# Attention into a soft mixture of experts: a new order of the last weight tiles, a finer warming-up, and one normalisation moved from VectorE to ScalarE

## The chip, the cores and the metric

The kernel runs on one core of a Trainium2 chip. The core has five engines, each with its own instruction queue: TensorE (PE, matmuls and their weight loads), VectorE (DVE), ScalarE (ACT), GpSimd (POOL) and SyncE (SP), which here issues nearly all DMA transfers. The metric is the device time of one execution in microseconds (us); lower is better. Times inside an execution are counted from the start of its span.

## The reference

Attention over 8 batches of 8 heads with 576 tokens and 64 channels, and a soft mixture of experts on its output:

```python
q_rot, k_rot = rotate(q), rotate(k)
scores = scale * q_rot @ k_rot.T
attn = softmax(scores)            # over keys, 1e-9 added to the sum
x = (attn @ v) -> (4608, 512)     # 8 x 576 tokens, 8 heads x 64
logits = x @ phi                  # 32 slots, 4 for each of 8 experts
d = softmax(logits, over tokens)
slot_input = d.T @ x
slot_out[e] = relu(slot_input[e] @ w1[e]) @ w2[e]     # 512 -> 1024 -> 512
out = softmax(logits, over slots) @ slot_out
```

The arrays are float32. The two softmaxes over the logits need all tokens of all batches (the one over tokens) or can be done batch by batch (the one over slots).

## The kernel before, in words

**Attention.** The 64 heads are worked off as 32 pairs, numbered 0 to 31; four pairs make a batch. A pair's q and k come in (`x_in`), are multiplied by cosines and sines on GpSimd (line 226), added on VectorE, and split into a high and a low float16 half (`hl`). PE multiplies them once for the row maxima (line 281, reduced on VectorE, line 283) and once for the scores (line 357), ScalarE takes the exponential into `a_t` and `a_tr` (lines 358, 376, 377), and PE multiplies that with V (line 392), whose last column of ones gives the sums. `o_out` copies the result to `o_sb`, `recip` takes one over the sums, and `norm` multiplies by it on GpSimd (line 441) into `xn`, the tokens of the batch.

**Order.** The order in which these steps are emitted is written out by hand: the list `FRONT`, then times in `EARLY` and `WHEN`. A step's time has no unit and only sorts the steps; each engine then works through its own instructions in that order, waiting on semaphores. GpSimd and SP follow the same order. Pair 29's `norm` stands at 141.9, after pair 30's at 140.1.

**The end of attention.** `release_att` closes the memory pools of attention and lays eleven weight tiles of 512 KB, `wt0` to `wt10`, over them; `FREED` is the order in which they are loaded. By the order of the pools `wt0` and `wt1` lie over the two `o_sb` and pair 30's `v_in`, `wt2` over pair 31's `v_in` and the first `a_t`, `wt3` to `wt6` over the four `a_t`, `wt7` over the last `a_t`, `a_tr` and pair 30's `hl`, `wt8` and `wt9` over the `hl` of pairs 30 and 29, and `wt10` over that of pair 31. SP issues one load after the other, so a load whose memory is still in use holds up those behind it. The weights themselves come in the same order whichever tile they go to.

Then the pairs of the last batch are transposed (`natural`, line 465: nine transposes a pair, into a bank each), copied to `xt` (`natural_out`, line 485) and multiplied with phi (line 491). Pair 31 is normalised straight from PSUM by `norm_last`, all on VectorE, its last 64 queries of each head by line 456; `natural_last` (lines 474 to 477) transposes it into the bank that `natural_out(30)` has emptied and a second one.

**Experts.** Statistics of the last batch and the update of the slot inputs (lines 526 to 908), the two layers (`ffn1_steps`, line 921, and `ffn2_steps`, line 943), and the combination with the tokens' weights (line 973), whose results go out from line 976 on.

**Warming-up.** While the first loads run, `heat` sends matmuls to PE whose result nobody reads: 21 of 288 columns, each with its own weight load (line 737). A second call sends 16 more.

Of the kernel before, what the change touches and what calls it, by code (L numbers as in the profile page):

```python
# [26 lines left out]
HC = S // 2  # L27
# [12 lines left out]
)  # L40
N_WARM = 21
N_ROW = 2
FIRST = 1
N_COLD = 3
# [9 lines left out]
N_HL = 3  # L54
N_XN = 1
WIDE = True
FREED = (9, 8, 10, 3, 4, 5, 6, 0, 1, 7, 2)
PACE = {("m_rows", 29): 3, ("m_rows", 30): 3, ("m_rows", 31): 1}
WHEN = {
    "load0": (-18.089368, -21.237240, -19.262252, -19.815526), "spin0": (-18.026370, -19.323083, -15.395919,  # L60
# [88 lines left out]
}  # L149
QL, QH, KH, KL = range(4)  # L150
TERMS = ((KH, QH), (KH, QL), (KL, QH), (None, None))
# [3 lines left out]
def attn_softmoe(ctx, tc, qk, v, phi, w1, w2, cs, ident, sel, seg, out):  # L155
    nc = tc.nc
# [22 lines left out]
    rows = (slice(0, 64), slice(64, P))  # L179
# [7 lines left out]
    lift = const.tile([P, P], F16, name="lift")  # L187
# [21 lines left out]
    halves = {}  # L209
# [43 lines left out]
    def bank2(k=None):  # L253
        if k is None:
            k = min((i for i in range(N_S) if age[i] is not None), key=lambda i: age[i])
        age[k] = None
        t = ps[k].tile([P, 2, 512], F32, name=f"s_ps{k}")
        held[id(t)] = k, t
        return t

    def free(t):
        k, _ = held.pop(id(t))
        age[k] = next(ages)
# [120 lines left out]
    def av(p, i):  # L384
        if i == 0:
            os_[p] = bank2()
            left_av[p] = NB + 1
        o, vt, at = os_[p], vts[p], ats.pop((p, i))
        left_av[p] -= 1

        def unit(lhs, c, h, u, v):
            nc.tensor.matmul(o[rows[c], h, VW * u:VW * u + VW], lhsT=lhs, rhs=v, start=(i == 0 and u == 0),  # L392
                             stop=(left_av[p] == 0 and u == 3 + (c == h)))

        if i < NB:
            for c, h, u in [(c, h, u) for u in range(4) for h in range(2) for c in range(2)] + [(0, 0, 4), (1, 1, 4)]:
                q = 256 if u == 4 else 64 * u + 320 * c
                unit(at[:, h, q:q + 64], c, h, u, vt[:, 2 * i + h])
        else:
            for u in range(5):  # L400
                for c in range(2):
                    for r in range(2 if u < 4 else 1):
                        q = 256 if u == 4 else 64 * u + 320 * c
                        q += 64 * (r ^ c)
                        unit(at[rows[r], q:q + 64], c, r ^ c, u, vt[rows[r], 2 * NB + c])
# [37 lines left out]
    def norm_last(p):  # L443
        t = os_.pop(p)
        free(t)
        o = t[:, :, 0:5 * VW].rearrange("p h (u x) -> p h u x", x=VW)
        rr, pp = rrs[p % 2], p % NP
        nc.vector.tensor_scalar_add(out=rr[:, :, 0:4], in0=o[:, :, 0:4, 64], scalar1=1e-9)
        for h in range(2):
            nc.vector.tensor_scalar_add(out=rr[rows[h], h, 4:5], in0=o[rows[h], h, 4, 64:65], scalar1=1e-9)  # L450
        nc.vector.reciprocal(out=rr, in_=rr)
        xn = xns[p // NP][:, :, pp * P:(pp + 1) * P].rearrange("p j (h x) -> p h j x", h=2)
        nc.vector.tensor_tensor(out=xn[:, :, 0:4], in0=o[:, :, 0:4, 0:64],
                                in1=rr[:, :, 0:4].unsqueeze(3).broadcast_to([P, 2, 4, 64]), op=ALU.mult)
        for h in range(2):
            nc.vector.tensor_scalar_mul(out=xn[0:64, h, 4], in0=o[rows[h], h, 4, 0:64], scalar1=rr[rows[h], h, 4:5])

    def natural(p, k=None):
        b, pp = divmod(p, NP)
# [21 lines left out]
    def natural_out(p):  # L481
        xts[p] = xt = late.tile([P, S], F32, name="xt", bufs=N_X)
        t = flat.pop(("n", p))
        free(t)
        nc.scalar.copy(out=xt, in_=t.rearrange("p n x -> p (n x)")[:, 192:192 + S])  # L485
# [160 lines left out]
    def load_w(pool, bufs, tag="w_exp", pace=None, wt=None):  # L646
        n = order[len(w_tiles)]
        layer, rest = divmod(n, 4 * E)
        if wt is not None:
            wt = wt.rearrange("p (c x) -> p c x", c=4 if layer else 2)  # L650
        elif layer == 0:
            wt = pool.tile([P, 2, 512], F32, name=tag, bufs=bufs)
        else:
            wt = pool.tile([P, 4, 256], F32, name=tag, bufs=bufs)
        if pace is nc.vector:
            pace.memset(wt[0:1, 0, 0:1], 0.0)
        elif pace:
            before = w_tiles[order[len(w_tiles) - 2]]
            pace.tensor_copy(out=wt[0:1, 0, 0:1], in_=before[0:1, 0, 0:1])
        nc.sync.dma_start(out=wt.rearrange("p c x -> p (c x)"), in_=(w1, w2)[layer][rest])  # L660
        w_tiles[n] = wt
# [13 lines left out]
    def release_att():  # L675
# [5 lines left out]
        wt.append(tl.tile([P, 1024], F32, name="wt10"))  # L681
        for i in FREED:
            load_w(None, 1, wt=wt[i])
# [46 lines left out]
        plan[f"t{i}"] = lambda p, i=i: score(p, i)  # L730
    for i in range(NB + 1):
        plan[f"av{i}"] = lambda p, i=i: av(p, i)
    def heat(n):
        cold = bank2()
        free(cold)
        for _ in range(n):
            nc.tensor.matmul(cold[:, 0, 0:HC], lhsT=lift, rhs=halves[0][:, KH, 0:HC], start=True, stop=True)

    def small_loads(p):
        nc.sync.dma_start(out=phi_sb, in_=phi.rearrange("(c p) n -> p c n", p=P))  # L740
        nc.sync.dma_start(out=sel_sb, in_=sel)

    plan.update({
        "heat": lambda p: heat(16),
        "small_loads": small_loads,
        "join0": lambda p: join(p, 0),
# [23 lines left out]
            high(0, t, c)  # L770
    done.update((n, 0) for n in ("spin0", "spin1", "join", "high0", "high1", "load0", "load1"))
    done.update((n, 1) for n in ("join0", "join1"))
    heat(N_WARM)

    last = NPAIR - 1
    STEADY = {n: w if isinstance(w, tuple) else (w,) * NP for n, w in WHEN.items()}
# [26 lines left out]
    natural(last - 1, 1)  # L803
    natural(last - 3, 0)
    norm_last(last)
    for q in (last - 2, last - 1, last - 3):
        natural_out(q)
    lt = bank2(2)
    lp = lt[:, 0, 0:192]
# [28 lines left out]
    m, al, dt, xn = state["m"], state["al"], state["dt"], xns.pop(B - 1)  # L838
# [28 lines left out]
    for c in range(2):  # L867
        for j in range(4):
            nc.tensor.matmul(sh[c][32 * j:32 * j + 32], lhsT=dn[:, 32 * j:32 * j + 32],
                             rhs=xn[:, j, 256 * c:256 * c + 256], start=True, stop=True, tile_position=(0, 32 * j))  # L870
    for i in range(NP):
        nc.tensor.matmul(rp[32 * i:32 * i + 32], lhsT=dn[0:64, P + 32 * i:P + 32 * i + 32],
                         rhs=xn[0:64, 4, i * P:(i + 1) * P], start=True, stop=True, tile_position=(0, 32 * i))
# [32 lines left out]
    for _ in range(N_LEAD):  # L906
        load_w(wp, N_W)
    nc.vector.tensor_tensor(out=st[:, 0:256].rearrange("p (i e z) -> p i e z", i=NP, z=2 * SPE)[:, :, :, SPE:],
                            in0=fp[:, 0:P].rearrange("p (i e z) -> p i e z", i=NP, z=SPE),
# [171 lines left out]
```

## Time and profile before

| | us |
|---|---|
| median of 3 runs | 482.27 |
| lowest, highest run | 481.59, 484.14 |
| profiled execution, its own time | 483.52 |
| its span, first to last instruction | 481.7 |
| PE busy | 457.9 (95%) |
| VectorE, ScalarE, GpSimd busy | 374.9, 291.1, 289.8 |

The profiled execution is one run; its time is its span and what lies around it (1.8 us). Busy times are sums over the span. The chain that ended last is followed back from the last instruction to whatever released each one. "issue" is time in which an engine waited for nothing that the profile shows. `q8` is the DMA queue whose packets are called "instruction".

### The profile page before, as it was taken

To read this page: it belongs to the slowest core of one execution; us is meant where nothing else is said; L and a number is where in the kernel's file an instruction comes from. 1 tells how busy PE (TensorE), PEld (TensorE's weight loads), DVE (VectorE), ACT (ScalarE), POOL (GpSimd) and SP (SyncE) were. 2 spreads that over 40 slices of the span, in tenths; PEclk is the share of its full clock that TensorE was granted. 3 is DMA by queue.
4 is the path that set the end of the run, shared out by engine and by line. 5 is a ranking of instruction groups with operands and counts; after the bars stand their busy time and mean duration, and the time that the engine had idled before them with its cause. 6 is when DMAs were issued, how large, how long until landed. Compare 5 with 4: busy or idle time off the path is not lost.

```text
span 481.7 us, 24135 instructions
## 1 busy us (share of the span) xinstructions
PE 457.9 (95%) x10758; PEld 374.2 (78%) x10758; DVE 374.9 (78%) x630; ACT 291.1 (60%) x670; POOL 289.8 (60%) x321
## 2 busy tenths in 40 slices
PE   4699999999999999999999999999999999999992
PEld 2377888878888788878887888888878888853871
DVE  4998998878878887988899889988896864356443
ACT  2166767665676577657765776577666766632442
POOL 2897858947893778577866787687849301230000
PEclk9899999999999999999999999999999999999997
DMA  7545745472554356335543553444452044799898
GB/s 256 194 146 191 257 150 197 168 264 98 197 182 170 123 175 213 122 132 193 196 146 138 199 174 129 148 142 173 167 197 101 23 171 164 254 405 407 342 376 326
DMA packets 29707, 94.00 MB, mean 195 GB/s; under 512 B 5028, under 2 KB 6820, under 8 KB 29604
## 3 DMA queue, kind: packets, MB, share of 16 engines
q1 hardware_dynamic: 29604, 92.47, 53.8%
q8 instruction: 84, 1.38, 1.2%
q14 instruction: 19, 0.16, 0.1%
HBM read 82.95 MB, written 9.44 MB: 192 GB/s over the span
## 4 chain that ended last, share of the span: by engine, by line
PE 90%; DVE 4%; ACT 2%; DMA 1%; issue 1%; SPq 0%; DVEq 0%; ACTq 0%
PE s_ps L392 34%; PE s_ps L357 26%; PE s_ps L281 8%; PE s_ps L372 4%; PE o_ps L943 3%; PE o_ps L921 3%; PE s_ps L465 2%; PE s_ps L502 2%; PE c_ps L973 2%; PE s_ps L290 2%; DVE nm L283 1%; PE s_ps L562 1%; DMA x_in<-in_qk 1%; DVE hl L239 1%; DVE x_in L230 1%
## 5 line engine op out<-in xcount | busy, mean ns | idle before, releaser
L226 POOL TENSOR_TENSOR x_in<-x_in,cs_sb 128x288 f32<-128x288 f32 x248 | 236.8, 987 | 82.7 <-DMA x_in<-in_qk 61.1
L283 DVE TENSOR_REDUCE nm<-s_ps 128x2 f32<-128x576 f32 x256 | 187.6, 752 | 48.9 <-PE s_ps L281 47.7
L392 PEld LDWEIGHTS s_ps<-v_in,a_t 128*64 128x64 f32 x4608 | 139.2, 137 | 12.2 <-issue 4.5
L358 ACT ACTIVATE a_t<-s_ps 128x576 f32<-128x576 f32 x256 | 145.8, 660 | 4.0 <-PE s_ps L357 3.8
L392 PE MATMUL s_ps<-v_in,a_t 128*64 128x66 f32 x4608 | 146.3, 223 | 0.2 <-issue 0.2
L357 PE MATMUL s_ps<-hl 64*128 64x288 f16 x1536 | 133.2, 283 | 0.0
L357 PEld LDWEIGHTS <-hl 64*128 64x128 f16 x1536 | 79.2, 94 | 18.4 <-issue 8.0
L357 PE MATMUL s_ps<-peak,lift 64*128 64x288 f16 x512 | 75.3, 283 | 0.3 <-ACT peak L334 0.3
L281 PE MATMUL s_ps<-hl 64*128 64x288 f16 x512 | 67.0, 286 | 3.2 <-ACT hl L235 1.5
L423 ACT COPY o_sb<-s_ps 128x528 f32<-128x528 f32 x31 | 18.6, 600 | 75.2 <-PE s_ps L392 75.2
L441 POOL TENSOR_TENSOR xn<-o_sb,rr 128x640 f32<-128x640 f32 x31 | 39.7, 1290 | 33.2 <-PE s_ps L562 13.9
L235 ACT CAST hl<-x_in 128x576 f16<-128x576 f32 (+1 forms) x66 | 40.8, 657 | 22.7 <-DVE x_in L230 22.6
L239 DVE TENSOR_TENSOR hl<-x_in,hl 128x1152 f16<-128x1152 f32 x32 | 52.9, 1653 | 1.6 <-ACT hl L235 1.6
L230 DVE TENSOR_TENSOR x_in<-x_in 128x1152 f32<-128x1152 f32 (+1 forms) x35 | 47.4, 1355 | 0.1
L281 PEld LDWEIGHTS <-hl 64*128 64x128 f16 x512 | 29.1, 94 | 18.4 <-issue 7.9
L357 PEld LDWEIGHTS <-lift 64*128 64x128 f16 x512 | 27.0, 94 | 4.9 <-issue 0.5
L292 DVE TENSOR_REDUCE nm<-s_ps 128x2 f32<-128x576 f32 x32 | 24.0, 751 | 3.4 <-PE s_ps L290 3.4
L392 PE MATMUL s_ps<-v_in,a_tr 64*64 64x66 f32 x1152 | 26.4, 224 | 0.0
L392 PEld LDWEIGHTS s_ps<-v_in,a_tr 64*64 64x64 f32 x1152 | 21.9, 133 | 4.3 <-issue 3.5
L372 PE MATMUL s_ps<-hl 64*64 64x256 f16 (+1 forms) x384 | 24.1, 287 | 0.0
L485 ACT COPY xt<-s_ps 128x576 f32<-128x576 f32 x31 | 19.4, 651 | 5.0 <-PE s_ps L465 5.0
L376 ACT ACTIVATE a_tr<-s_ps 128x512 f32<-128x512 f32 x32 | 19.1, 598 | 4.7 <-PE s_ps L372 3.9
(184 smaller groups left out, 419.7 us busy)
## 6 DMA issues: line engine op xcount, KB each, us to landing
x_in<-in_qk SPq DMA_DIRECT2D x62, 576.0 KB
w_exp<-in_w SPq DMA_DIRECT2D x53, 512.0 KB
v_in<-in_v SPq DMA_DIRECT2D x32, 330.0 KB
out<-w_exp SPq DMA_DIRECT2D x16, 512.0 KB
wt<-in_w SPq DMA_DIRECT2D x11, 512.0 KB
peak<-mr SPq DMA_DIRECT2D x120, 0.5 KB
x_in<-in_qk SPq DMA_DIRECT2D x4, 288.0 KB
out<-w_exp SPq DMA_DIRECT2D x4, 256.0 KB
```

Source lines behind the costliest of these rows:

```text
L226: eng.tensor_tensor(out=x[:, :, c], in0=x[:, :, c], in1=cs_sb[:, :, c], op=ALU.mult)
L230: nc.vector.tensor_tensor(out=x[:, t, 0, c], in0=x[:, t, 0, c], in1=x[:, t, 1, c], op=ALU.add)
L235: nc.scalar.copy(out=halves[p][:, 1 + t, c], in_=loaded[p][:, t, 0, c])
L239: nc.vector.tensor_tensor(out=hl[:, 0:4:3], in0=x[:, :, 0], in1=hl[:, 1:3], op=ALU.subtract)
L281: nc.tensor.matmul(s[c, h, 0:HC], lhsT=hl[rows[h], QH, P * j + c.start:P * j + c.stop], rhs=hl[rows[h], KH, half[n]], start=True, stop=True)
L283: nc.vector.tensor_reduce(out=nm[:, n, j:8:4], in_=s[:, :, 0:HC], axis=AX.X, op=ALU.max, negate=True)
L292: nc.vector.tensor_reduce(out=nm[:, :, 8], in_=s[:, :, 0:HC], axis=AX.X, op=ALU.max, negate=True)
L357: nc.tensor.matmul(s[c, h, 0:HC], lhsT=lhs, rhs=rhs, start=(x == 0), stop=(x == 3))
L358: nc.scalar.activation(out=ats[p, b][:, :, half[n]], in_=s[:, :, 0:HC], func=AF.Exp, scale=SCALE)
L372: nc.tensor.matmul(s[rows[h ^ n], n, 0:w] if n else s[rows[h], 0, 512 - w:512], lhsT=lhs, rhs=rhs, start=(x == 0), stop=(x == 3))
L392: nc.tensor.matmul(o[rows[c], h, VW * u:VW * u + VW], lhsT=lhs, rhs=v, start=(i == 0 and u == 0), stop=(left_av[p] == 0 and u == 3 + (c == ...
L441: eng.tensor_tensor(out=xn, in0=t[:, :, :, 0:64], in1=rr.unsqueeze(3).broadcast_to([P, 2, 5, 64]), op=ALU.mult)
```

## The change

1. The first warming-up sends 29 matmuls of 209 columns in place of 21 of 288. The second call keeps its 16 of 288.
2. `FREED` becomes 9, 8, 0, 1, 10, 7, 3, 4, 5, 6, 2, and pair 29's `norm` is emitted at 129.0, before pair 30's and after the steps at 128.3.
3. In `norm_last` the last 64 queries of the second head are multiplied on ScalarE. `natural_out(29)` is emitted ahead of that multiply, so ScalarE's order is `natural_out(29)`, the multiply, `natural_out(30)`, `natural_out(28)`.

```diff
-N_WARM = 21
+N_WARM, W_WARM = 29, 209
...
-FREED = (9, 8, 10, 3, 4, 5, 6, 0, 1, 7, 2)
+FREED = (9, 8, 0, 1, 10, 7, 3, 4, 5, 6, 2)
...
-    ("av1", 31): 140.406591, ("norm", 29): 141.896775, ("av4", 31): 142.290391,
+    ("av1", 31): 140.406591, ("norm", 29): 129.000000, ("av4", 31): 142.290391,
...
-        for h in range(2):
-            nc.vector.tensor_scalar_mul(out=xn[0:64, h, 4], in0=o[rows[h], h, 4, 0:64], scalar1=rr[rows[h], h, 4:5])
+        nc.vector.tensor_scalar_mul(out=xn[0:64, 0, 4], in0=o[rows[0], 0, 4, 0:64], scalar1=rr[rows[0], 0, 4:5])
+        natural_out(p - 2)
+        nc.scalar.mul(out=xn[0:64, 1, 4], in_=o[rows[1], 1, 4, 0:64], mul=rr[rows[1], 1, 4:5])
...
-    def heat(n):
+    def heat(n, w=HC):
...
-            nc.tensor.matmul(cold[:, 0, 0:HC], lhsT=lift, rhs=halves[0][:, KH, 0:HC], start=True, stop=True)
+            nc.tensor.matmul(cold[:, 0, 0:w], lhsT=lift, rhs=halves[0][:, KH, 0:w], start=True, stop=True)
...
-    heat(N_WARM)
+    heat(N_WARM, W_WARM)
...
-    for q in (last - 2, last - 1, last - 3):
+    for q in (last - 1, last - 3):
         natural_out(q)
```

## Rows read from the trace of the kernel before

**Rows 1.** The page: busy time and instructions; DMA queue q8; chain's shares.

```profile
PE 457.9 (95%) x10758; PEld 374.2 (78%) x10758; DVE 374.9 (78%) x630; ACT 291.1 (60%) x670; POOL 289.8 (60%) x321
...
q8 instruction: 84, 1.38, 1.2%
...
PE 90%; DVE 4%; ACT 2%; DMA 1%; issue 1%; SPq 0%; DVEq 0%; ACTq 0%
PE s_ps L392 34%; PE s_ps L357 26%; PE s_ps L281 8%; PE s_ps L372 4%; PE o_ps L943 3%; PE o_ps L921 3%; PE s_ps L465 2%; PE s_ps L502 2%; PE c_ps L973 2%; PE s_ps L290 2%; DVE nm L283 1%; PE s_ps L562 1%; DMA x_in<-in_qk 1%; DVE hl L239 1%; DVE x_in L230 1%
```

**Rows 2.** Timeline of PE, 414 to 428: start, us, operation, count, idle before.

```profile
414.24 4.44 PE L392 MATMUL s_ps<-v_in,a_t 128*64 128x66 f32 x144
...
419.35 0.52 PE L465 MATMUL s_ps<-id_sb,xn 64*128 64x64 f32 x9
420.62 0.78 PE L465 MATMUL s_ps<-id_sb,xn 64*128 64x64 f32 x18 [0.76 <-issue]
...
421.83 0.52 PE L474 MATMUL s_ps<-id_sb,xn 64*128 64x64 f32 x9
...
427.36 0.41 PE L872 MATMUL t_ps<-xn,dn 64*32 64x128 f32 x5 [0.39 <-issue]
```

**Rows 3.** Windows: PE, PEld, DVE, ACT, POOL busy (instructions), clock, DMA share, GB/s.

```profile
420.62:427.36 6.74, 6.31 (x128) 4.42 (x128) 3.46 (x12) 4.10 (x16) 1.95 (x7) 1.00 0.99 393
```

**Rows 4.** DMA queues, 417.50 to 419.40: packets, MB, share of 16 engines.

```profile
q8 instruction: 1, 0.02, 5.8%
```

**Rows 5.** DMA queues, 425.0 to 426.2.

```profile
q8 instruction: 1, 0.02, 5.5%
```

**Rows 6.** Timeline, 100 to 102.

```profile
100.82 0.26 ACT L377 ACTIVATE a_tr<-s_ps 64x128 f32<-64x128 f32 x1
101.61 0.10 PEld L281 LDWEIGHTS <-hl 64*128 64x128 f16 x2 [1.32 <-issue]
```

**Rows 7.** DMA queues, 99.1 to 100.3.

```profile
q8 instruction: 1, 0.02, 5.0%
```

**Rows 8.** Timeline of SP, DMA issues, 95.5 to 98.

```profile
95.54 0.39 SPq L221 DMA_DIRECT2D x_in<-in_qk  x1
```

**Rows 9.** Windows (columns as in rows 3).

```profile
96.49:101.61 5.12, 4.00 (x132) 3.41 (x130) 4.66 (x7) 2.19 (x9) 1.90 (x3) 1.00 0.74 238
```

**Rows 10.** Timeline, 6.5 to 13.

```profile
6.84 4.70 PE L737 MATMUL s_ps<-hl,lift 128*128 128x288 f16 x21 [6.84 <-ACT hl L235]
...
12.75 0.74 DVE L283 TENSOR_REDUCE nm<-s_ps 128x2 f32<-128x576 f32 x1
```

**Rows 11.** Timeline of GpSimd, 398 to 416.

```profile
411.34 2.48 POOL L441 TENSOR_TENSOR xn<-o_sb,rr 128x640 f32<-128x640 f32 x2 [4.92 <-DVE rr L433]
```

**Rows 12.** Timeline of SP, single DMA issues, 405 to 415.

```profile
408.43 0.34 SPq L660 DMA_DIRECT2D w_exp<-in_w  x1
...
414.22 0.33 SPq L660 DMA_DIRECT2D wt<-in_w  x1
```

**Rows 13.** Timeline of ScalarE and VectorE, 419.3 to 423.

```profile
419.90 0.64 ACT L485 COPY xt<-s_ps 128x576 f32<-128x576 f32 x1 [3.83 <-PE s_ps L465]
...
420.82 0.57 DVE L456 TENSOR_SCALAR xn<-s_ps,rr 64x64 f32<-64x64 f32 x2
421.13 1.18 ACT L485 COPY xt<-s_ps 128x576 f32<-128x576 f32 x2 [0.59 <-PE s_ps L465]
```

**Rows 14.** ScalarE's groups by shape, 404 to 482: busy us, mean ns, idle before.

```profile
L425 ACT COPY o_sb<-s_ps 64x66 f32<-64x66 f32 x2 | 0.4, 209 | 0.0
```

**Rows 15.** Timeline of PE, 184.0 to 184.8.

```profile
184.66 0.34 PE L392 MATMUL s_ps<-v_in,a_t 128*64 128x66 f32 x5 [0.16 <-issue]
```

**Rows 16.** Windows (columns as in rows 3).

```profile
18.00:20.00 2.00, 1.93 (x11) 1.00 (x10) 2.00 (x4) 0.00 (x0) 1.08 (x2) 0.50 0.94 351
20.00:22.00 2.00, 2.00 (x13) 1.23 (x10) 2.00 (x3) 1.19 (x2) 1.83 (x2) 0.72 1.04 402
22.00:24.00 2.00, 1.93 (x19) 1.38 (x20) 1.90 (x6) 0.06 (x1) 1.86 (x4) 1.00 0.49 193
```

## The prediction

> **What bounds the kernel now.** I read the page first. TensorE (PE) is busy 95% of the span, and the chain that ended last is 90% PE; the whole DMA share of that chain is 1%, and one entry, the first load of x_in, accounts for it [rows 1]. So no weight tile and no output is waited for in the tail. A change of load order can pay only if it makes PE's own chain shorter. Then I went through PE's timeline for places where PE stands still though nothing that the program waits for is late ("issue"). The two in the tail stand before the 10th transpose of line 465 (0.76 us) and in the middle of line 872 (0.39 us) [rows 2]. The reader should see how far apart they are: from the end of the first to the end of the second PE runs 128 matmuls and 128 weight loads, 256 instructions [rows 3]. The page gives the reason for that number: 10,758 matmuls and as many weight loads, 21,516 instructions, against 84 "instruction" packets of 1.38 MB, which is 256 instructions and 16 KB a packet [rows 1]. PE's program itself comes by DMA in blocks of 256, and PE stalls where a block is late.
>
> The DMA table dates the packets. One fills most of 417.5 to 419.4: 5.8% of 16 engines over 1.9 us is 1.76 us [rows 4]. The next lies in 425.0 to 426.2 and takes 5.5% of 16 times 1.2 us, 1.06 us [rows 5]. PE goes on at 420.62 and 427.36 [rows 2], about 1.25 us after each has ended. The second was due for asking when PE entered the block before, at 420.62, and started only around 425.0: in between the DMA engines were 0.99 busy with weights [rows 3]. A block waits behind weight packets. That is the way by which this change can act.
>
> A third stall shows the same in mid-kernel: PE stands until 101.62. There its next bank was free only when ScalarE's a_tr ended at 100.82 + 0.26 = 101.08, so the block cost 101.61 - 101.08 = 0.53 us [rows 6]. Its packet (5.0% of 16 times 1.2, 0.96 us) lies in 99.1 to 100.3 [rows 7], behind an x_in load issued at 95.54; PE had entered the block before at 96.49, 256 instructions and the few that the window's edges cut in two earlier [rows 8, 9].
>
> **Part 1, the warming-up.** 21 matmuls of 288 columns are 6,048 columns; 29 of 209 are 6,061, 13 more, which is 0.01 us at either clock. Before, they took 4.70 us, until 11.54 [rows 10]. If instead every extra matmul cost as much as a whole old one, 4.70 / 21 = 0.22, the burst would be 8 x 0.22 = 1.8 us longer; if it cost nothing, it would be as long as now. [...] The cover is VectorE, which takes up line 281's bank only at 12.75, 1.2 us after the burst [rows 10]: it hides that much of a longer one, so the upper bound would cost 0.6 us, and without the cover 1.8.
>
> What does act is the count: 8 more matmuls with their loads are 16 more instructions ahead of everything else, so each block of PE's program now ends 16 instructions, 8 matmuls, earlier in the code.
>
> **Part 2, norm 29 earlier on GpSimd, and the weight tiles.** Before, norm(30) and norm(29) run back to back on GpSimd, 2.48 us from 411.34, because norm(30) stood first [rows 11]. Now norm(29) runs when its reciprocal is done, and norm(30) ends at 411.34 + 1.24 = 412.58. GpSimd's own later work comes 1.24 us sooner, and nobody waits for it: price 0, with that slack as cover. SP's issues before: a last ordinary tile at 408.43, two of the eleven right behind it, one at 414.22, and eight more up to 422 [rows 12]. wt0 and wt1 lie over o_sb and over pair 30's v_in, so in the new order they go out at about 412.6 and 413.0, wt10 again at about 414.2. wt7 lies over a_tr, which the last score-times-V matmuls read until the first transpose at 419.35 [rows 2]; SP is in order, so 3, 4, 5, 6 and 2 stand behind it and go out from about 419.4 to 422, as late as before. By 419.4 one tile more is moved. Nothing waits for that tile. What matters is that the DMA engines have nothing to move between about 417.7 and 420.6, just when PE's program is wanted.
>
> **Part 3, the split of line 456.** VectorE loses one of two multiplies, 0.57 / 2 = 0.28 us [rows 13]. ScalarE gains one of 64 x 64 from PSUM with a per-partition factor. The nearest row is the 64 x 66 copy, 0.21 us [rows 14]; the slowest it could plausibly be is half of VectorE's pair, 0.28. I take 0.25. [...] The multiply stands between natural_out(29) and natural_out(30); it waits for the reciprocal (ready at 420.2) and behind it wait natural_out(30), natural_out(28) and the last copy. Is VectorE on the path today? No: line 474 reuses the bank that natural_out(30) empties, at 421.13 + 0.59 = 421.72, and starts at 421.83; VectorE's second multiply had ended at 421.39 [rows 2, 13]. So the saved 0.28 is worth nothing as things stand, and the added 0.25 was hidden only in ScalarE's 0.59 us of idleness before 421.13, which the stall at 419.87 makes.
>
> **The sum in the tail.** After the shift the block border lies behind the first transpose, at 419.4. Call R the time at which PE goes on. Eight transposes (0.5), natural_out(29) (0.64), the multiply (0.25), natural_out(30) (0.59) and 0.1 to line 474 give R + 2.1, against 421.83 now: break-even is R = 419.7. The block is asked for 8 x 4.44 / 144, about 0.25 us, earlier [rows 2]; ahead of it are wt0, wt1 and wt10, at 0.52 MB / 393 GB/s = 1.33 us each [rows 3] behind the three loads issued from 408.43 on. With 1 us and more from an issue to its first packet (the x_in of 95.54 was ahead of a block asked for at 96.49) those run until about 413.7, so these until 417.7 [rows 8, 9, 12]. It starts at about 417.6, now alone, takes 1.0 instead of 1.76, and R = 418.6 + 1.25 = 419.85. Bounds: R = 419.35 if it is queued ahead of wt10 (no stall, 0.35 gained), 420.5 if it starts 0.65 us later (0.8 lost). I take +0.15. The next block is asked for about 0.8 us earlier, with one to three tiles ahead instead of a full line, and should be there before line 869 needs it near 426: -0.39, bound 0.
>
> **The sum elsewhere.** At 101 us the asking moves 16 instructions earlier, into the logits matmuls, 0.5 us, to about 0.45 us after the issue of x_in instead of 0.95 (96.49 - 95.54) [rows 8, 9]; that load's packets are then not yet on the engines, so the block gets ahead of them: -0.53, bound +0.4 if it does not. Four other borders show small stalls, such as 0.16 us at 184.66 [rows 15]; there the block can be needed 0.25 us earlier than it comes. Each changes by -0.2 to +0.25; I take +0.3 for the four. Sum: 0.15 - 0.39 - 0.53 + 0.3 = -0.47 us.
>
> The profiled run took 483.52 us, of which 481.7 are span and 1.8 lie around it; the median is 482.27, 1.25 lower. The terms are differences, so I apply them to the median: 481.8.
>
> **Rivals.**
> (a) The block comes in time before the transposes too. For it: the DMA engines are free from 417.7. Against: three tiles in a row end just then. Tail -0.35 - 0.39, elsewhere -0.23: 481.3.
> (b) Slower: the stall moves inside natural(29), where the multiply is no longer hidden, and R is 420.5; the blocks at 101 us and at the four small borders stay behind x_in and each costs what the shift takes. It decides against the change from R = 419.7 on. +0.8 - 0.39 + 0.4 + 0.3 gives 483.4.
> (c) Slower by more: 29 short matmuls do not raise PE's granted clock as 21 long ones did. Today it stands at 0.50 from 18 to 20 us, 0.72 over the next 2 us and 1.00 after [rows 16]. Were it half until 24 us, the 0.88 us of full speed in 20 to 22 and the 1.93 us busy in 22 to 24 would double: +2.8, 485.1. Against it: the columns and the start are the same.
> (d) Nothing: blocks are hidden whatever their borders, and what is saved on VectorE and spent on ScalarE is off the path: 482.3. The stalls 256 instructions apart [rows 2, 3] speak against it. [...]
>
> **How the numbers follow.** Forecast 0.48, (a) 0.17, (b) 0.20, (d) 0.10, (c) 0.05. The forecast's own range, from its four terms, is 481.2 to 482.6. The range runs from a little under (a) to (b), 480.9 to 483.4, and leaves (c) and some of the ends of (a) and (b) out. A measurement of this kernel can tell about 0.5%, 2.4 us, from no change (three runs of it span 2.5). Only (c) passes that on the slow side (0.05); nothing priced here does on the fast side, and I leave 0.03 for stalls that I have not listed. Same: 0.92.
>
> **What would show it.** Right: no "issue" before line 281 near 101 us; the stall of the last transposes sits behind the first one, not the ninth, and ends near 419.85; none in line 872; wt issues at 412.6, 413.0 and 414.2, then none until 419.4; weights landed over 1 us sooner with no effect at the end. Wrong: stalls at the old places in the code, which would refute the shift by 16; a granted clock that rises later than 21 us; an output phase that gets shorter with the weights, which would mean that DMA bounds the tail after all.

## The result, and the profile after

The change makes the kernel slower: 485.48 us median (482.54 to 489.22, 20 runs) against 482.41 (480.57 to 488.59, 20 runs) of before beside it, a ratio of 1.0062, 95% interval 1.0044 to 1.0080, 3.1 us. Ratios, here and below, are not the quotient of the two medians and leave out a few disturbed runs, so they can differ a little from it.

The profile after was taken of the fastest of the 20 executions, 482.54 us; it holds only a part of the loss. The page of the kernel after, to set beside [rows 1] (busy time, queue of PE's program, shares of the chain that ended last):

```profile
PE 457.4 (95%) x10766; PEld 375.4 (78%) x10766; DVE 375.2 (78%) x629; ACT 291.4 (61%) x671; POOL 290.8 (60%) x321
...
q8 instruction: 84, 1.38, 1.2%
...
PE 89%; DMA 2%; ACT 2%; DVE 2%; POOL 2%; issue 1%; SPq 1%; DVEq 0%; ACTq 0%; POOLq 0%
```

PE still bounds the kernel; eight matmuls more are the whole difference in its work. The timeline of PE in the tail, which answers to [rows 2]:

```profile
416.61 0.81 PE L392 MATMUL s_ps<-v_in,a_tr 64*64 64x66 f32 x36
417.35 0.27 PE L466 MATMUL s_ps<-id_sb,xn 64*128 64x64 f32 x1
418.94 1.08 PE L466 MATMUL s_ps<-id_sb,xn 64*128 64x64 f32 x26 [1.32 <-issue]
420.13 0.54 PE L492 MATMUL s_ps<-xt,phi_sb 128*32 128x128 f32 x16
421.13 0.52 PE L475 MATMUL s_ps<-id_sb,xn 64*128 64x64 f32 x9 [0.46 <-ACT xt L486]
...
426.00 0.42 PE L873 MATMUL t_ps<-xn,dn 64*32 64x128 f32 x8
```

The stall among the transposes has moved from behind the ninth to behind the first, as the shift of the block borders by eight matmuls wants it, but it is 1.32 us and not shorter than the 0.76 of [rows 2]. A second wait stands before line 475, 0.46 us for ScalarE. The stall in the middle of line 872 (now 873) is gone. The granted clock stays at 1.00 behind the stall in this execution (columns as in [rows 3]):

```profile
418.94:424.10 5.16, 4.59 (x112) 3.88 (x111) 1.15 (x4) 3.46 (x10) 0.00 (x0) 1.00 0.98 370
```

The DMA table of 416.5 to 417.7 dates the block (queue: packets, MB, share of 16 engines), as [rows 4] did before:

```profile
q8 instruction: 1, 0.02, 5.0%
```

5.0% of 16 times 1.2 us is 0.96 us. It came behind the tiles. The timeline of SP from 409 to 415, and of GpSimd and ScalarE (to [rows 11, 12, 13]):

```profile
410.48 2.22 SPq L661 DMA_DIRECT2D wt<-in_w  x3
```

```profile
404.23 1.26 POOL L441 TENSOR_TENSOR xn<-o_sb,rr 128x640 f32<-128x640 f32 x1
409.19 1.26 POOL L441 TENSOR_TENSOR xn<-o_sb,rr 128x640 f32<-128x640 f32 x1 [3.70 <-DVE rr L433]
```

```profile
419.44 0.64 ACT L486 COPY xt<-s_ps 128x576 f32<-128x576 f32 x1 [5.51 <-PE s_ps L466]
420.11 0.31 ACT L457 ACTIVATE xn<-s_ps,rr 64x64 f32<-64x64 f32 x1
```

Pair 29's norm is done 5 us before pair 30's, and three tiles go out in one bunch, 6.9 us before the first transpose. Windows of the kernel after over this stretch (columns as in [rows 3]):

```profile
410.00:412.00 2.00, 2.00 (x36) 1.53 (x30) 0.67 (x2) 2.00 (x5) 0.91 (x2) 1.00 1.01 393
412.00:414.00 2.00, 2.00 (x64) 1.91 (x62) 0.04 (x1) 1.93 (x4) 0.34 (x1) 1.00 0.83 279
414.00:416.00 2.00, 2.00 (x75) 2.00 (x73) 0.46 (x1) 0.00 (x0) 0.00 (x0) 1.00 0.95 350
```

The DMA engines are 0.83 to 1.01 busy until 416: the line that the block stood in. Near 101 us, where before PE stood until 101.62 [rows 6], the timeline of PE shows no wait at all:

```profile
99.14 0.42 PE L281 MATMUL s_ps<-hl 64*128 64x288 f16 x4
99.49 1.27 PE L392 MATMUL s_ps<-v_in,a_t 128*64 128x66 f32 x36
100.70 0.43 PE L290 MATMUL s_ps<-hl 64*64 64x288 f16 x4
101.06 0.54 PE L357 MATMUL s_ps<-hl 64*128 64x288 f16 x6
```

So this one execution shows 0.6 us more stall among the transposes and 0.5 more wait before line 475, 0.5 us less at 101 us and 0.4 less in line 872, and a span 0.9 us shorter than in the profile of before. What the typical execution loses had to be found by experiments.

### The profile page after: what moved, and what is told of

Its sections match the earlier page's. It is cut to its first block, busy times and chain, and to the rows that moved or that the text cites. A ratio compares the mean times of both kernels' runs of the same rounds, so it can differ in the third digit from the quotient of the medians.

```text
span 480.8 us, 24152 instructions
## 1 busy us (share of the span) xinstructions
PE 457.4 (95%) x10766; PEld 375.4 (78%) x10766; DVE 375.2 (78%) x629; ACT 291.4 (61%) x671; POOL 290.8 (60%) x321
## 4 chain that ended last, share of the span: by engine, by line
PE 89%; DMA 2%; ACT 2%; DVE 2%; POOL 2%; issue 1%; SPq 1%; DVEq 0%; ACTq 0%; POOLq 0%
PE s_ps L392 35%; PE s_ps L357 26%; PE s_ps L281 8%; PE s_ps L372 4%; PE o_ps L922 3%; PE o_ps L944 3%; PE s_ps L503 2%; PE s_ps L466 2%; PE s_ps L290 2%; POOL x_in L226 2%; DMA x_in<-in_qk 1%; PE c_ps L974 1%; PE s_ps L563 1%; DMA out<-w_exp 1%; DVE x_in L230 1%
## 5 line engine op out<-in xcount | busy, mean ns | idle before, releaser
L230 DVE TENSOR_TENSOR x_in<-x_in 128x1152 f32<-128x1152 f32 (+1 forms) x35 | 48.5, 1386 | 0.5 <-POOL x_in L226 0.4
```

What stands on the lines that cost most here:

```text
L230: nc.vector.tensor_tensor(out=x[:, t, 0, c], in0=x[:, t, 0, c], in1=x[:, t, 1, c], op=ALU.add)
```

## The experiments

Each kernel ran 12 times, beside before on the same chip. "Tail" is the span less the start of the first of the last transposes (line 465 or its successor), both from the kernel's one trace: before 481.7 - 419.35 = 62.4. "Stall" is PE's wait among these transposes in that trace. "Clock" is the median of the mean granted clock of the 12 runs, and "low" counts runs with 0.987 or less.

| run | edit | median | before | ratio (95%) | clock, low | tail | stall |
|---|---|---|---|---|---|---|---|
| e1 | before itself | 481.45 | 481.79 | 0.9988 (0.9964 to 1.0013) | 0.9905, 2 | 61.4 | 0 |
| e2 | warming-up alone | 481.48 | 481.79 | 0.9997 (0.9980 to 1.0014) | 0.988, 5 | 61.7 | 0 |
| e4 | 16 instructions alone | 481.70 | 481.79 | 1.0004 (0.9980 to 1.0027) | 0.990, 1 | 61.7 | 0 |
| e7 | norm 29 alone | 481.57 | 481.93 | 0.9994 (0.9972 to 1.0015) | 0.991, 2 | 61.3 | 0 |
| e6 | ScalarE's multiply alone | 481.69 | 481.93 | 1.0012 (0.9989 to 1.0034) | 0.9905, 2 | 62.1 | 0 |
| e8 | change, old tile order | 482.46 | 481.93 | 1.0006 (0.9983 to 1.0028) | 0.989, 2 | 62.0 | 0 |
| e12 | tile order alone | 484.73 | 482.46 | 1.0042 (1.0013 to 1.0071) | 0.9865, 9 | 64.0 | 1.71 |
| e5 | tile order and norm 29 | 483.51 | 481.93 | 1.0025 (0.9999 to 1.0051) | 0.989, 5 | 64.2 | 1.85 |
| e3 | change, old warming-up | 483.86 | 481.79 | 1.0043 (1.0012 to 1.0074) | 0.987, 7 | 64.4 | 1.85 |
| e9 | the change | 484.88 | 482.46 | 1.0044 (1.0015 to 1.0074) | 0.9855, 10 | 64.5 | 1.68 |
| e10 | change, two tiles ahead | 482.96 | 482.46 | 0.9997 (0.9972 to 1.0021) | 0.990, 2 | 62.5 | 0.23 |
| e13 | e10, all on VectorE | 482.28 | 482.21 | 1.0004 (0.9980 to 1.0028) | 0.989, 4 | 62.8 | 0.10 |
| e11 | before, pause by hand | 484.57 | 482.46 | 1.0050 (1.0021 to 1.0079) | 0.986, 9 | 64.5 | 1.51 |
| e14 | before, half the pause | 482.56 | 482.21 | 1.0014 (0.9995 to 1.0032) | 0.990, 2 | 62.4 | 0.85 |

### Which third of the change: e1 to e4

My first theory, CLOCK, was that the short warming-up matmuls leave the clock low (rival (c) of the prediction): the 20 runs after have a median clock of 0.986, and the slowest have 0.978 and 0.983. Its rivals: BLOCKS, the shifted borders of PE's program fall in worse places; TAIL, one of the edits in the tail makes the end longer.

**e1**, before against itself.

> The kernel before against itself, for the scatter of its time and for its mean granted clock in each run, which the timed runs of before do not list. Every theory: ratio 1.000 within 0.002, median near 482.4. If the clock is the cause (theory CLOCK), its mean granted clock lies clearly above that of the changed kernel (median 0.986 over 20 runs), and its slow runs are those of low clock. If the cause lies in blocks or in the tail (BLOCKS, TAIL), the two kernels have clocks alike.

Ratio 0.9988; median clock 0.9905 in place of 0.986. The clock does differ between the kernels, so BLOCKS and TAIL as I had put them, with clocks alike, were both incomplete.

**e2**, the finer warming-up alone:

```diff
-N_WARM = 21
+N_WARM, W_WARM = 29, 209
...
-            nc.tensor.matmul(cold[:, 0, 0:HC], lhsT=lift, rhs=halves[0][:, KH, 0:HC], start=True, stop=True)
+            nc.tensor.matmul(cold[:, 0, 0:w], lhsT=lift, rhs=halves[0][:, KH, 0:w], start=True, stop=True)
...
-    heat(N_WARM)
+    heat(N_WARM, W_WARM)
```

> The kernel before with the finer warming-up alone (29 matmuls of 209 columns). CLOCK (the short matmuls change when PE runs at half its clock) and BLOCKS (the 16 more instructions move the borders of PE's program to worse places): the whole of the change, +3 us, 485.4. TAIL (the weights' order, the earlier norm of pair 29 and ScalarE's multiply make the end longer): 0, 482.4.

0.9997, and the interval leaves no more than 0.2% either way. CLOCK, in the place where I had put it, and BLOCKS fall as the cause of 3 us. Five of the 12 runs have a low clock, so a small effect on the clock isn't excluded.

**e4**, the shift alone, as eight matmuls of 16 columns behind the old 21:

```diff
-    def heat(n):
+    def heat(n, tiny=0):
...
+        for _ in range(tiny):
+            nc.tensor.matmul(cold[:, 0, 0:16], lhsT=lift, rhs=halves[0][:, KH, 0:16], start=True, stop=True)
...
-    heat(N_WARM)
+    heat(N_WARM, 8)
```

> The kernel before with its 21 long warming-up matmuls and 8 more of 16 columns behind them: 16 more instructions, as in the change, but the old burst for the clock. BLOCKS: +3, 485.4. CLOCK: about 0, 482.4, since the burst is the old one. TAIL: 482.4. My own forecast's account of the blocks would give less than before: -0.53 at 101 us and something around zero in the tail, 482.

1.0004, between 0.9980 and 1.0027: no cost of the shift by itself is to be seen, and not the 3 us of BLOCKS.

**e3**, the change with the old warming-up:

```diff
-N_WARM, W_WARM = 29, 209
+N_WARM, W_WARM = 21, 288
```

> The changed kernel with the old warming-up (21 matmuls of 288 columns), so the new order of the tiles, norm 29 earlier and the multiply on ScalarE alone, with the borders of PE's program where they were. CLOCK and BLOCKS: 482.4, and a stall again before line 281 near 101 us. TAIL: 485.4.

1.0043: the loss is in the tail. The trace says how. Timeline of PE of e3, and windows over the stall and over what follows it:

```profile
418.22 0.52 PE L466 MATMUL s_ps<-id_sb,xn 64*128 64x64 f32 x9
420.60 0.98 PE L466 MATMUL s_ps<-id_sb,xn 64*128 64x64 f32 x18 [1.85 <-issue]
...
423.03 1.84 PE L492 MATMUL s_ps<-xt,phi_sb 128*32 128x128 f32 x48
```

```profile
418.22:420.60 2.38, 0.53 (x13) 0.45 (x10) 1.47 (x6) 0.95 (x2) 0.00 (x0) 1.00 0.53 174
420.99:424.41 3.42, 3.42 (x74) 2.92 (x73) 0.42 (x1) 1.60 (x3) 0.00 (x0) 0.50 0.79 261
```

PE stands for 1.85 us, and 0.4 us after it goes on its granted clock falls from 1.00 to 0.50 for 3.42 us. The timeline of e2 over the same code, old order of tiles, has neither:

```profile
417.48 1.14 PE L465 MATMUL s_ps<-id_sb,xn 64*128 64x64 f32 x27
418.73 0.54 PE L491 MATMUL s_ps<-xt,phi_sb 128*32 128x128 f32 x16
419.27 0.77 PE L474 MATMUL s_ps<-id_sb,xn 64*128 64x64 f32 x9
419.97 1.21 PE L491 MATMUL s_ps<-xt,phi_sb 128*32 128x128 f32 x48
421.11 0.34 PE L546 MATMUL s_ps<-id_sb,l_sb 64*128 64x64 f32 x4
```

The new theory, TILES-CLOCK: the tiles delay the block, the stall costs its own length, and then the clock takes more.

### Which part of the tail: e5 to e8

**e5**, tile order and norm 29, on the kernel before:

```diff
-FREED = (9, 8, 10, 3, 4, 5, 6, 0, 1, 7, 2)
+FREED = (9, 8, 0, 1, 10, 7, 3, 4, 5, 6, 2)
...
-    ("av1", 31): 140.406591, ("norm", 29): 141.896775, ("av4", 31): 142.290391,
+    ("av1", 31): 140.406591, ("norm", 29): 129.000000, ("av4", 31): 142.290391,
```

> The kernel before with two edits of the change: the new order of the weight tiles and pair 29's norm moved ahead of pair 30's. Old warming-up, both multiplies on VectorE. Theory TILES-CLOCK: wt0, wt1 and wt10 now go out before PE's next block of program is wanted, the block waits behind them, PE stands 1.3 to 1.9 us among the transposes of line 465, and after the stall its granted clock falls to 0.50 for 3.4 us as it did at 420.99 to 424.41 in the run of the changed kernel with the old warming-up, which costs 1 to 1.7 us more: 1.3 - 0.8 + 1.5 = about +2, 483.8 to 484.5, and a median clock below that of before (0.990). Rival ACT: ScalarE's multiply stands on PE's path and is the loss; this kernel then runs as before, 481.8.

483.51, a little less than expected; its interval just reaches 1 and only 5 of its 12 runs have a low clock, so the timed runs alone would not decide. The trace has the stall (1.85 us) and the fall of the clock, windows of e5:

```profile
422.86:426.27 3.41, 3.41 (x57) 3.08 (x58) 0.96 (x3) 1.27 (x7) 0.00 (x0) 0.50 0.92 342
```

**e6**, ScalarE's multiply alone:

```diff
-        for h in range(2):
-            nc.vector.tensor_scalar_mul(out=xn[0:64, h, 4], in0=o[rows[h], h, 4, 0:64], scalar1=rr[rows[h], h, 4:5])
+        nc.vector.tensor_scalar_mul(out=xn[0:64, 0, 4], in0=o[rows[0], 0, 4, 0:64], scalar1=rr[rows[0], 0, 4:5])
+        natural_out(p - 2)
+        nc.scalar.mul(out=xn[0:64, 1, 4], in_=o[rows[1], 1, 4, 0:64], mul=rr[rows[1], 1, 4:5])
...
-    for q in (last - 2, last - 1, last - 3):
+    for q in (last - 1, last - 3):
```

> The kernel before with ScalarE's multiply alone. TILES-CLOCK: within 0.5 us of before, 481.8, no stall of over 1 us in the transposes and a median clock of 0.990. ACT: +2 us, 483.9.

1.0012, no stall, clock 0.9905. ACT as the main cause falls, yet the multiply isn't free. PE's and ScalarE's timelines of e6:

```profile
416.57 1.14 PE L466 MATMUL s_ps<-id_sb,xn 64*128 64x64 f32 x27
417.82 0.54 PE L492 MATMUL s_ps<-xt,phi_sb 128*32 128x128 f32 x16
419.38 0.52 PE L475 MATMUL s_ps<-id_sb,xn 64*128 64x64 f32 x9 [1.02 <-ACT xt L486]
```

```profile
417.13 0.64 ACT L486 COPY xt<-s_ps 128x576 f32<-128x576 f32 x1 [3.83 <-PE s_ps L466]
418.35 0.31 ACT L457 ACTIVATE xn<-s_ps,rr 64x64 f32<-64x64 f32 x1 [0.58 <-DVE xn L455]
418.68 1.18 ACT L486 COPY xt<-s_ps 128x576 f32<-128x576 f32 x2
```

ScalarE stands 0.58 us at the multiply until VectorE is through, then takes 0.31, and natural_out(30), for whose bank line 475 waits, comes that much later: PE waits 1.02 us. In the tails of e6 and e8 0.5 us of it is left (62.1 and 62.0 against 61.3 to 61.7 in e1, e2, e4, e7).

**e7**, norm 29 alone, on the kernel before, and **e8**, the change with the old order of tiles:

```diff
-    ("av1", 31): 140.406591, ("norm", 29): 141.896775, ("av4", 31): 142.290391,
+    ("av1", 31): 140.406591, ("norm", 29): 129.000000, ("av4", 31): 142.290391,
```

```diff
-FREED = (9, 8, 0, 1, 10, 7, 3, 4, 5, 6, 2)
+FREED = (9, 8, 10, 3, 4, 5, 6, 0, 1, 7, 2)
```

> The kernel before with pair 29's norm moved ahead of pair 30's on GpSimd and nothing else; the tiles keep their old order. TILES-CLOCK: within 0.5 us of before, 481.8; the tiles 0 and 1 still stand behind 10, 3, 4, 5 and 6. If the earlier norm itself is what costs (it could hold up GpSimd's rotation or pair 30's norm), +2, 483.9.

> The changed kernel with the old order of the tiles alone put back. TILES-CLOCK: all of the loss gone, 481.8 within 0.7 us, median clock 0.990. Rival, that several parts cost something each (ACT, the norm, the shift of the borders together): 483 to 485.

0.9994 and 1.0006: no cost of the earlier norm is to be seen, and with the old order alone put back the loss is gone.

### The mechanism: e9 to e12

**e9**, the change once more, without an edit.

> The changed kernel as it is, beside the next three on one chip, for its ratio there and for a second trace of it: the one at hand is of its fastest execution. TILES-CLOCK: ratio 1.005 to 1.008, a stall of 1.3 us or more behind the first transpose and, in this trace, the granted clock at 0.50 for some 3.4 us from about 420 on. If the clock stays at 1.00 after the stall and the time is nevertheless 484 or more, the fall of the clock isn't what makes its typical run longer than its fastest.

1.0044, a little under what I expected. Its trace is of the typical kind that the first profile was not. PE's timeline, and windows behind the stall:

```profile
418.12 0.27 PE L466 MATMUL s_ps<-id_sb,xn 64*128 64x64 f32 x1
420.07 1.30 PE L466 MATMUL s_ps<-id_sb,xn 64*128 64x64 f32 x26 [1.68 <-issue]
...
422.27 0.79 PE L475 MATMUL s_ps<-id_sb,xn 64*128 64x64 f32 x9
...
424.66 0.34 PE L547 MATMUL s_ps<-id_sb,l_sb 64*128 64x64 f32 x4
```

```profile
420.76:424.17 3.41, 3.31 (x65) 2.73 (x65) 0.42 (x1) 2.38 (x5) 0.00 (x0) 0.50 1.03 418
```

**e10**, one tile fewer ahead of the block:

```diff
-FREED = (9, 8, 0, 1, 10, 7, 3, 4, 5, 6, 2)
+FREED = (9, 8, 0, 1, 7, 10, 3, 4, 5, 6, 2)
```

> The changed kernel with tile 10 behind tile 7, which has to wait for the first transposes. So two tiles (0 and 1) go out at about 410.5 and 411 and not a third, and the DMA line ends some 1.3 us sooner. TILES-CLOCK: the block of PE's program is there before the transposes, or the stall is under 0.7 us and the clock stays up; at least half of the loss is gone, 482.0 to 483.3. If the loss has to do with what lies in the tiles or with the multiply on ScalarE and not with the line ahead of the block: as the changed kernel, 485.

0.9997. Same border, same multiply, a stall of 0.23 us, clock at 1.00. PE's timeline of e10:

```profile
418.18 0.27 PE L466 MATMUL s_ps<-id_sb,xn 64*128 64x64 f32 x1
418.68 1.08 PE L466 MATMUL s_ps<-id_sb,xn 64*128 64x64 f32 x26 [0.23 <-issue]
...
420.98 0.52 PE L475 MATMUL s_ps<-id_sb,xn 64*128 64x64 f32 x9 [0.57 <-ACT xt L486]
```

The windows of 416 to 418 of e9 and then of e10, both just ahead of the same code, show the line that is gone (DMA share 0.86 and 0.25):

```profile
416.00:418.00 2.00, 2.00 (x86) 1.93 (x82) 0.00 (x0) 0.00 (x0) 0.00 (x0) 1.00 0.86 336
```

```profile
416.00:418.00 2.00, 2.00 (x84) 1.93 (x82) 0.00 (x0) 0.00 (x0) 0.00 (x0) 1.00 0.25 96
```

**e11**, a pause made by hand in the kernel before; two maxima and one small matmul are added, with results that nobody else reads:

```diff
+    pz = small.tile([P, 2], F32, name="pz", bufs=1)
+    first = flat["n", last - 2].rearrange("p n x -> p (n x)")[:, 192:192 + S]
+    for k in range(2):
+        nc.vector.tensor_reduce(out=pz[:, k:k + 1], in_=first, axis=AX.X, op=ALU.max)
-    natural(last - 1, 1)
+    natural(last - 1, 1, pz)
...
-    def natural(p, k=None):
+    def natural(p, k=None, pause=None):
...
+        if pause is not None:
+            nc.tensor.matmul(t[0:2, 0:2], lhsT=pause, rhs=pause, start=True, stop=True)
```

> The kernel before, old order of tiles, with a pause of PE made by hand and no DMA in it: after the first nine transposes VectorE does two maxima over that bank (2 x 0.74 us), and a two-column matmul that reads them stands ahead of the tenth transpose. PE stands some 1.7 us there. If a stall of this length is enough to make the granted clock fall: 0.50 for 3.4 us after it in part of the runs, a median clock below 0.989, and a time 1.7 us and 1 to 1.7 us more, 484 to 485. If the clock falls only for a stall that comes of missing instructions: the clock stays 0.990, and the time is 482.5 to 483.5, the pause alone.

1.0050, as slow as the change, with the old order of tiles and no late block there. Timeline and windows of e11:

```profile
419.25 0.19 PE L463 MATMUL s_ps<-pz 128*2 128x2 f32 x2 [1.51 <-DVE pz L808]
```

```profile
420.82:424.23 3.41, 3.29 (x62) 2.71 (x62) 0.92 (x3) 0.72 (x2) 0.00 (x0) 0.50 0.99 382
```

Here the granted clock falls to 0.50 for 3.41 us behind a wait of 1.51 us for VectorE, as in e9 behind one of 1.68 us for a block, and 9 of the 12 runs have a low clock, where e9 has 10: in these two traces the fall came behind the standing still, whichever of the two PE waited for.

**e12**, the order alone, on the kernel before:

```diff
-FREED = (9, 8, 10, 3, 4, 5, 6, 0, 1, 7, 2)
+FREED = (9, 8, 0, 1, 10, 7, 3, 4, 5, 6, 2)
```

> The kernel before with the new order of the tiles alone; pair 29's norm stays behind pair 30's. Tiles 0 and 1 can then go out only after that norm, near 413.8, some 3 us later than in the changed kernel, with tile 10 right behind, so the line of three tiles ends near 418 in place of 416.6. TILES-CLOCK: the block comes later still, a stall of 1.5 us or more in the transposes with the clock falling behind it, 483.5 to 485. If the order does harm only together with the earlier norm: 481.8.

1.0042, stall 1.71 us, clock 0.50 behind it. The tiles went out at 413.63, 3 in a row, as the timeline of SP shows:

```profile
413.63 1.28 SPq L660 DMA_DIRECT2D wt<-in_w  x3
```

So the order needs no help from the norm.

### The two open prices: e13 and e14

**e13** is e10 with the multiply back on VectorE (the diff of e6 the other way round); **e14** is e11 with one maximum in place of two:

```diff
...
-    for k in range(2):
-        nc.vector.tensor_reduce(out=pz[:, k:k + 1], in_=first, axis=AX.X, op=ALU.max)
-    natural(last - 1, 1, pz)
+    nc.vector.tensor_reduce(out=pz[:, 0:1], in_=first, axis=AX.X, op=ALU.max)
+    natural(last - 1, 1, pz[:, 0:1])
```

> The changed kernel with tile 10 behind tile 7 and both last multiplies back on VectorE; so the finer warming-up, the earlier norm of pair 29 and two tiles ahead of the block. If ScalarE's multiply costs what PE waits before line 475 in the run with two tiles (0.57 us): 482.4 on a chip where before is 482.5, ratio 0.998 to 1.000, and no such wait. If the multiply is hidden: the ratio of the run with two tiles, 1.000. A gain of 0.5% over before is expected by nobody.

1.0004. The wait before line 474 is gone, but the time doesn't show it. Its one trace spends more elsewhere, on another block that came late, in line 943 of PE's timeline:

```profile
457.20 0.41 PE L943 MATMUL o_ps<-w_exp,l_sb 128*32 128x128 f32 x3 [0.94 <-issue]
```

So the multiply's price, 0.5 us by the tails, stays under what 12 runs tell apart, and no version here beats the kernel before.

> The kernel before with a pause half as long: one maximum (0.74 us) in place of two between the first nine transposes and the tenth, so PE stands some 0.8 us. If the fall of the clock needs the longer stall: clock at 1.00 in the tail of this trace, a median clock of 0.989 to 0.990 and a ratio of 1.000 to 1.002. If any stall there makes the clock fall: median clock 0.986, as with the pause of 1.5 us, and a ratio of 1.003 to 1.005.

1.0014, clock 0.990. PE's timeline and a window behind the pause of e14:

```profile
420.33 0.19 PE L463 MATMUL s_ps<-pz 128*1 128x1 f32 x2 [0.85 <-DVE pz L807]
```

```profile
420.33:424.20 3.87, 3.75 (x100) 3.18 (x101) 2.45 (x10) 2.34 (x5) 0.00 (x0) 1.00 0.97 357
```

In these two traces 0.85 us left the clock at 1.00 and 1.51 us did not. Between e14 and e11 the tail grows by 2.0 us for 0.66 us more of waiting; between the first trace after (1.32 us, clock 1.00, tail 63.4) and e9 (1.68 us, clock 0.50, tail 64.5) by 1.0 us for 0.36. What is left over, 0.7 to 1.4 us, is an estimate of the price of the clock; the lower end is low, because the first trace after also waits 0.46 us before line 475 and e9 doesn't.

## Why the prediction was wrong

**The loss.** I forecast a gain of 0.5 us; the change is 3.1 us slower by the medians of its 20 runs, 2.4 by those of e9. The tails give about as much: without a stall and with both multiplies on VectorE 61.5 us (mean of e1, e2, e4, e7); the tile order adds 2.6 (e5 and e12, mean 64.1); the multiply alone adds 0.5 (e6, e8). The change's own tail in e9 is 64.5; there PE doesn't wait before line 475, so the stall covers most of the multiply and the two don't simply add. Each tail is one execution; the 45 runs of 68 with a clock of 0.987 or less in the five sets with the full new order, against 22 of 108 in the nine without it and without the long pause, show that a fall of the clock is more frequent with the order. One fall of 3.4 us to half the clock is 3.4 x 0.5 / 482 = 0.0035 of the mean clock, the step from 0.990 to 0.9865. A longer early stretch at half clock lowers it too (the profiled runs of e1, with 6.83 us of it, and of e6, with none, have mean clocks of 0.987 and 0.993; last section), so the low clock of a single run doesn't say where it fell.

**The step that failed** is the sum in the tail, "R = 419.85 ... I take +0.15", with its break-even of R = 419.7. It let the path from the first transpose to the last ones (line 474, now 475) grow by 0.15 us. In e9 this path takes 422.27 - 418.12 = 4.15 us, in e2, with the old order, 419.27 - 417.48 = 1.79, so it grows by 2.36. The block and the base make up that (0.15 + 1.45 + 0.69 = 2.29); the clock adds more behind it:

- The block, 1.45 us. On the clock of the trace R looks right: PE goes on at 420.07 in e9, and 419.85 was forecast. That is luck, since in e9 everything up to there runs 1.2 us earlier than in [rows 2]. Counted from PE's first transpose, R was to come 0.5 us behind (419.85 - 419.35) and came 1.59 behind in the first trace after and 1.95 in e9. So PE stood 1.32 and 1.68 us, not about 0.2. The issues were not late. The three tiles, 1.57 MB, were: the sum took them at 393 GB/s, 4.0 us, while in the first trace after the windows from 412 to 416 show 279 and 350; at their mean it is 5.0 us, an estimate that accounts for 1.0 of the 1.1 us of that trace. Why they moved more slowly wasn't tried.
- The base, 0.69 us. [Rows 2] have a stall of 0.76 us already, and I took the path from 419.35 to line 474 at 421.83, 2.48 us, as that of before. Of five traces with before's tail it is the only one with such a stall, and with one in line 872. So a typical before had no stall to exchange, neither this one nor the 0.39 us, and the profiled run's 1.25 us above the median, which I carried along as an offset, was a warning.
- The clock. Nothing in the sum allowed for it. Its fall takes another 0.55 us behind line 475 (to line 547, 424.66 - 422.27 = 2.39 us in e9; to line 546, 421.11 - 419.27 = 1.84 in e2), and its whole price is the 0.7 to 1.4 us above. Rival (c) named a clock that stays low, at 0.05, but put it into the warming-up, where the time of e2 shows nothing; it acts behind the stall.

Rival (b) had the place and the sign right, a stall inside natural(29), with R at 420.5, 1.15 us behind the first transpose. It was too small by the rest of the block, by the base and by the clock: 483.4.

**Part 1** was right: no price to be seen (e2), and the shift of the borders too. That the burst would be as long as before no run shows: 29 matmuls of 209 columns took 4.09 us in the first trace after and 5.23 in that of e2, where 21 of 288 took 4.70 [rows 10]. Of nine traces with the old border at 101 us five show PE waiting there for 0.3 us or more (the first, e1, e5, e7, e14), of seven with the shift none. The 0.53 us is not to be seen in the ratios of e2 and e4.

**Part 2.** Norm 29's price of 0 was right as far as e7 can tell. The issues came as forecast relative to PE: three tiles from 6.9 us before the first transpose (412.6 against 419.35 is 6.8), then none until it. No wait for that tile shows, and what it delays was mis-sized: the stall is 0.23 us with two tiles ahead (e10) and 1.3 to 1.9 with three.

**Part 3.** The multiply took 0.31 us, not 0.25. Its cover was to be ScalarE's idleness made by the stall; without the stall it stands on PE's path, as e6 shows, behind VectorE's other multiply, a wait that I had left out.

**Rival (d)** had the blocks hidden whatever their borders. At this border four of five traces with before's tail agree with it, and all five with the full new order don't (1.32 to 1.85 us): here it held mostly where the tiles went out one by one, nearly where two went out together (0.23 us, e10), and not where three did.

## What to carry to other kernels

Loads that nobody waits for need not be free to move earlier: here they stood ahead of PE's own program, and three 512 KB tiles in place of two turned a fetch that cost 0.2 us into 1.3 to 1.9 us of standing still. Count such a delay from an event of the same engine, not on the clock of another execution's trace. Price a stall of PE by its length and by what the clock does behind it (in e9 3.41 us at 0.50), and look at the mean clock of all runs, since a single profile may be of an execution that was spared. Take the base of a sum from more than one trace where its stalls may come and go: a gain that consists of removing a stall which the typical run hasn't got is none.

## What the runs showed that I had not expected

A pause of 1.51 us on PE, between stretches in which it was busy throughout, was followed by 3.41 us at half its clock, and one of 0.85 us was not (e11, e14); the 1.32 us of the first trace after was spared, while 1.68 to 1.85 in four others were not.

The early stretch at half clock [rows 16] changes from execution to execution with the same program. Windows of e1, which is the kernel before, and of e6, which differs from it only in the tail:

```profile
15.62:22.45 6.83, 6.01 (x30) 2.88 (x31) 6.26 (x11) 1.25 (x2) 5.73 (x8) 0.50 0.79 283
```

```profile
15.00:19.00 4.00, 3.05 (x27) 2.07 (x27) 3.64 (x6) 0.00 (x0) 3.77 (x6) 1.00 0.85 286
```

Once 6.83 us at 0.50, once none, where [rows 16] had about 3.4; the 16 traces have 6.83 three times (e1, e4, e5), none once (e6), and about 3.4 otherwise. The spans of the two executions were 482.4 and 478.7 us. How much of that difference is the clock's wasn't tried.
